# A softmax-free attention and a gated layer on one core: a PSUM bank opened one unit sooner, the loads of v one period later, one weight sum on another engine

## The chip, the cores and the metric

The kernel runs on one core of a Trainium2 chip. The metric is the time of one execution in device microseconds (us), as the median of several runs. A core has TensorE (PE in the profile, its weight loads PEld), VectorE (DVE), ScalarE (ACT), GpSimd (POOL) and SyncE (SP). SP, ACT and POOL issue DMA transfers, each in the order of its own queue; 16 DMA engines carry them out.

## The reference

The first half is a linear attention with decay over q, k and v of shape 4 x 8 x 768 x 64 (batch, heads, sequence, head size). Per head, with a decay `lam` near 1:

```python
intra = np.einsum('bhic,bhjc->bhij', qb, kb) * Dmask[None]   # Dmask: lam ** (i - j) for i >= j, else 0
intra = np.einsum('bhij,bhjd->bhid', intra, vb)
inter = np.einsum('bhid,bhde->bhie', qb * lam_pow[None], kv_state)
out[:, :, sl] = intra + inter
kv_state = lam_block * kv_state + np.einsum('bhsd,bhse->bhde', kb_dec, vb)
```

Its output, as 3072 tokens of 512, goes through a layer: `h = x @ w_in` (512 x 2048), `g = h * tanh(softplus(h))` (Mish), `g @ w_out` (2048 x 512). All inputs and the output are float32.

## The kernel before

**Staging.** The sequence is cut into 6 groups of 128 positions; a group holds four batch entries, so 512 tokens. A chunk, numbered i = 4 n + b, is one batch entry b of group n: k, q and v of 128 positions in 8 heads. `load_k`, `load_q` and `load_v` (lines 61 to 78) fetch a chunk through POOL's queue and convert it to float16. k and q have 8 buffers each; v has 8 fixed tiles `vz`, so group n shares its tiles with group n - 2. `scale_k` (L265) multiplies k by its decay to `ktil`; `turn` (L269) makes `ktil` and transposes q and `ktil` by DMA on SP's queue (L274, `qraw` and `kraw`).

**Periods and units.** The program is an order written out by hand: every engine works through its own instructions as the Python code emits them. Period n holds the layer of group n and, laid between its pieces, the attention of group n + 1. The unit is the piece of the layer's work. Period 0 has its own loop (L741), periods 1 to 5 that at L776. In a unit, the code first emits the unit's matmuls, then a load, sums on DVE, a turn, and the attention step that `visit` names.

- *Units 0 to 13 of periods 2 to 5* make h. `mm1_duo` (L422) computes a block of 2 x 128 features by 256 tokens with 8 matmuls into one of two `ph` banks, and ACT applies Mish (L441). Half 0 of the tokens is in units 0 to 5, half 1 in units 6 to 13. The last 512 features are computed as seven products of quarters and of their sums (`set_unit`, L506): P1 in unit 4, P2 in 5, P5 and P6 in 10, P7 and P3 in 12, P4 in 13. P5 has the bank `sw`; P6, P7 and P4 share `sz`; P3 has `sy`. The step `open` (L546) takes the banks of `sw` and `sz` and has ACT copy P1's result, kept in SBUF as `u1`, into `sz` (L548), onto which P6 adds. After P5 ACT keeps its result as `p5` (L539), and after P6 it copies `sz` to `sy` (L564). The seven sums of `x_sum` (four on DVE, L496) and `in_sum` are the operands.
- *The following 14 units* make the output: seven products again, two units each (`fast_unit`, L663), with operands `gsum` (L589) and `tsum` (L461). `tsum` is made once, in period 0, by `weight_sum`: four sums of quarters of w_out in two halves each, seven of these on DVE and the last, `weight_sum(3, 1)`, on POOL (L765). Period 1 has plain units 0 to 15 instead of 0 to 13, so its output is in units 16 to 29.

**PSUM.** Tags name banks: `ph` and `po` have two each, `pS`, `pk`, `pO` and `pq` one. `sw` and `sz` are the two `po` banks. So are, in unit 6, two of the four banks of scores of `pair_s` (L338); DVE frees them by masking the scores into `sb` (L365), those two first.

**The attention in the periods.** `pair_s` computes scores of two chunks of group n + 1 from `qraw` and `kraw` (L349), `pair_o` (L368) multiplies them with v (L376), scales them on DVE to `xtok` (L384) and transposes that by DMA on SP's queue to `xt` (L386), the layer's input of the next period. Chunks 0 and 1 are in units 6 and 14 and give half 0; chunks 2 and 3 are in units 24 and 27, and give half 1, which unit 6 of the next period reads. `pair_a` (units 3 and 19) updates the state. In period 0 `look_t`, `look_s` and `look_o` do the same with transposes on PE (L211), in the last 7 units; the transposes of k and one of the banks of scores share the bank `pk`.

**The loads.** In period 0, behind unit 25, 26 and 27, two loads each of group 2 are emitted; `scale_k(7)` on POOL stands behind those of unit 26. In period n = 1, 2, 3 the list `later` holds the twelve loads of group n + 2 and gives one at each unit of `slots`. Ahead of each, `pace` (L396) has POOL copy one element of what ACT wrote last, so that POOL can't run ahead.

Of the kernel before, what the change touches and what calls it, by code (L numbers as in the profile page):

```python
# [20 lines left out]
def kernel(  # L21
# [10 lines left out]
    nc = tc.nc  # L32
    B, H, S, D = q.shape
    C = 128
    NG = S // C
# [21 lines left out]
    def chunk_rows(t, i):  # L57
        n, b = divmod(i, B)
        return t[b, :, n * C : (n + 1) * C, :].rearrange("h p c -> p h c")
# [17 lines left out]
    def load_v(i):  # L77
        nc.gpsimd.dma_start(out=vz[i % NVB][:, :, 0:D], in_=chunk_rows(v, i))  # L78
# [218 lines left out]
    def look_kv(i, tag="po"):  # L297

        n, b = divmod(i, B)
        pv = ps.tile([128, JP, 128], F32, name="pv", tag=tag, bufs=2 if tag in ("po", "ph") else 1)  # L300
        for j in range(JP):
            nc.tensor.matmul(
                pv[:, j, :].rearrange("p (a e) -> p a e", a=2),
                ktil[i][:, 2 * j : 2 * j + 2, :].rearrange("p h c -> p (h c)"),
                vz[i % NVB][:, 2 * j : 2 * j + 2, 0:D],
                start=(j == 0), stop=(j == JP - 1), skip_group_check=True,
            )
        if n == 0:
            return lambda: nc.vector.tensor_tensor(out=wst[b], in0=pv, in1=lbm, op=ALU.mult)
        return lambda: sum_rows(n, b, pv, 0, JP, lambda rs: wst[b][rs, :, rs])  # L310
# [84 lines left out]
    def pace():  # L395
        nc.gpsimd.tensor_copy(paced, mark[-1])  # L396
# [49 lines left out]
    tsum = [const.tile([128, HK, HN], F16, name=f"tsum{i}") for i in range(4)]  # L446

    def w_quarter(r, c, s):

        return wout[2 * r + s][:, :, c * HN : (c + 1) * HN]  # L450

    def weight_sum(i, s, engine=None):

        ks = slice(s * NKI // WS, (s + 1) * NKI // WS)
        a, b, op = (
            (w_quarter(0, 1, s), w_quarter(0, 0, s), ALU.subtract),
            (w_quarter(1, 1, s), tsum[0][:, ks, :], ALU.subtract),
            (w_quarter(1, 1, s), w_quarter(0, 1, s), ALU.subtract),
            (w_quarter(1, 0, s), tsum[1][:, ks, :], ALU.subtract),
        )[i]  # L460
        (engine or nc.vector).tensor_tensor(out=tsum[i][:, ks, :], in0=a, in1=b, op=op)  # L461

    KH = NKC // 2
    SU = NKI - 4
# [109 lines left out]
    def token_sum(n, i, part):  # L574

        if (n, i) not in gsum:
            gsum[n, i] = work.tile([128, HK, 2 * C], F16, name=f"gsum{i}", tag=f"gsum{i}", bufs=1)
        w = HK // 2
        ks = slice(part * w, part * w + w)
        kh = slice(HK + part * w, HK + part * w + w)  # L580
        h = hsg[n]
        lo, hi = slice(0, 2 * C), slice(2 * C, 4 * C)
        a, b, op = (
            lambda: (h[:, ks, hi], h[:, kh, hi], ALU.add),
            lambda: (gsum[n, 0][:, ks, :], h[:, ks, lo], ALU.subtract),
            lambda: (h[:, ks, lo], h[:, ks, hi], ALU.subtract),
            lambda: (h[:, kh, lo], gsum[n, 1][:, ks, :], ALU.subtract),
        )[i]()
        nc.vector.tensor_tensor(out=gsum[n, i][:, ks, :], in0=a, in1=b, op=op)  # L589
# [146 lines left out]
    units = [(mm1_unit, (0, ni)) for ni in range(NKI)]  # L736
# [4 lines left out]
    for u, (fn, args) in enumerate(units):  # L741
        put_off = []
        fn(*args, **({"then": put_off} if u in (23, 25) else {}))
        if u < B - 1:
            look_kv(u + 1, "pq" if u == 0 else "po")()
        if 8 <= u < 8 + NVB - B:
            nc.vector.memset(vz[u - 8 + B][:, :, D : 2 * D], 0.0)
        elif u == 13:
            nc.vector.tensor_scalar(out=maskT, in0=rel, scalar1=0.0, scalar2=None, op0=ALU.is_ge)
        for i, s in {14: ((0, 0),), 15: ((0, 1),), 18: ((1, 0), (2, 0)),  # L750
                     20: ((1, 1), (2, 1))}.get(u, ()):
            weight_sum(i, s)
        for i, part in sums.get(u, ()):
            token_sum(0, i, part)
        if u == 8:
            for i in range(4):
                in_sum(i)
        if u == 22:
            scale_k(4)
            weight_sum(3, 0)  # L760
        then = [f(i, "po" if i == 5 else "ph") if f is look_kv else f(i) for f, i in visit.get(u, ())]
        if u == 23:
            scale_k(5)
            scale_k(6)
            weight_sum(3, 1, nc.gpsimd)  # L765
        for f in put_off + then:
            if f:
                f()
        if u in (25, 26, 27):
            for _ in range(2):  # L770
                ahead.pop(0)()
        if u == 26:
            scale_k(7)
    next_state(1, 0)

    for n in range(1, NG):  # L776
        r, s, t = Pair(), Pair(), Pair()
        r.n, r.bs, s.n, s.bs, t.n, t.bs = n, (2, 3), n + 1, (0, 1), n + 1, (2, 3)
        visit = {}
        d = 0 if n == 1 else 2  # L780
        if 1 < n < NG - 1:
            visit[3] = pair_a, r
        if n < NG - 1:
            visit[6 if d else 11] = pair_s, s
            visit[16 - d] = pair_o, s
            visit[26 - d] = pair_s, t
            visit[29 - d] = pair_o, t
        if n < NG - 2:
            visit[21 - d] = pair_a, s
        turns = {23 - d: (n + 2) * B, 25 - d: (n + 2) * B + 1}  # L790
        turns.update({3: (n + 1) * B + 2, 5: (n + 1) * B + 3} if d else {1: 9, 4: 10, 7: 11})

        def duo(g, half):
            return mm1_duo, (n, g, half * (GT // 2), (half + 1) * (GT // 2))

        def part(step):
            return set_unit, (n, step)

        if d:
            units = [[duo(g, 0)] for g in range(4)]  # L800
            units += [[part("P1"), duo(4, 0)], [part("P2"), duo(5, 0)]]
            units += [[duo(g, 1)] for g in range(3)] + [[duo(3, 1), part("open")]]
            units += [[part("P5"), part("P6")], [duo(4, 1)], [part("P7"), part("P3")], [duo(5, 1), part("P4")]]
        else:
            units = [[duo(g, half)] for half in range(2) for g in range(NKI // 2)]
        steps = ("P1", "P5", "P6", "P2", "P7", "P3", "P4")
        units += [[(fast_unit, (n, step, blk))] for step in steps for blk in range(2)]
        later = []
        if n < NG - 2:
            later = [(lambda f=f, i=(n + 2) * B + b: f(i)) for f, b in (  # L810
                (load_k, 0), (load_q, 0), (load_k, 1), (load_q, 1), (load_k, 2), (load_q, 2),
                (load_v, 0), (load_v, 1), (load_k, 3), (load_q, 3), (load_v, 2), (load_v, 3))]
        if d:
            slots = *range(6, 14), 15, 17, 19, 21
            sums = {13: ((0, 0), (0, 1), (1, 0), (1, 1)), 17: ((2, 0),), 18: ((2, 1),), 20: ((3, 0),), 21: ((3, 1),)}
        else:
            slots = *range(8, 16), 17, 19, 21, 23
            sums = {9: ((2, 0),), 11: ((2, 1),), NKI - 3: ((0, 0), (1, 0)), NKI - 1: ((0, 1), (1, 1)),
                    NKI + 4: ((3, 0),), NKI + 5: ((3, 1),)}
        for u, calls in enumerate(units):  # L820
            for fn, args in calls:
                fn(*args)
            if n == 1 and u == 0:
                turn(8)
                look_s(7)
            if n == 1 and u == 2:
                f = look_kv(7)
                look_o(7)
                f()
                next_state(1, 1)  # L830
            for _ in range({0: 1, 1: 1, 2: 2, 3: 1, 4: 1}.get(u, 0) if n == 1 else 0):
                pace()
                ahead.pop(0)()
            if later and u in slots:
                pace()
                later.pop(0)()
            for i, part in sums.get(u, ()):
                token_sum(n, i, part)
            if turns.get(u, NG * B) < NG * B:
                turn(turns[u])  # L840
            if d and u == 6:
                x_sum(n, 0)
            if u in visit:
                f, s_ = visit[u]
                s_.spare = ("po", "po") if u < 12 else ("pS", "pk") if f is pair_a else ("ph", "po")
                f(s_)
            if d and u == 6:
                for i in range(1, 4):
                    x_sum(n, i)
# [30 lines left out]
```

## Time and profile before

| | us |
|---|---|
| median of 3 runs | 205.01 (204.87 to 205.74) |
| the profiled execution | 206.21 |
| its span, from the first to the last instruction | 204.4 |
| PE busy | 191.2 (94%) |
| DVE busy | 141.8 (69%) |
| ACT busy | 99.0 (48%) |
| POOL busy | 82.2 (40%) |

The granted clock of PE is at full speed over the whole span. A row of the timeline has the start, the duration, engine and line, operation, what it writes and reads (`ph<-xt,win`), the shapes, the count, and in brackets how long the engine stood idle before it and what ended that. Rows with a count merge several instructions. Matmuls overlap, so a row of 8 matmuls that lasts 1.04 us gives way to the next after some 0.87. Starts are in us from the beginning of the span.

### The profile page before, as it was taken

Reading aid. Unit: us, or ns where it says so; the run is one execution under the profiler, and the core shown is the slowest. Engines: PE = TensorE matmul, PEld = TensorE weight load, DVE = VectorE, ACT = ScalarE, POOL = GpSimd, SP = SyncE. Lnnn points to the kernel's source line nnn. Section 1 sums busy time; section 2 is a strip of 40 time slices with the busy share of each in tenths; the row PEclk is TensorE's granted clock in tenths of the full one; section 3 lists DMA queues with packets and bytes.
Section 4 is the critical chain, followed back from the end, with each engine's and each line's share of the span. In section 5 each row is a group of like instructions: output and inputs, shape, how many; then the busy total and the mean of one; then the engine's idle time right before and its main releaser. Section 6 shows DMA issues by size and latency. Waiting matters only on the chain. (4 is left out here: it accounts for less than half of the span.)

```text
span 204.4 us, 5076 instructions
## 1 busy us (share of the span) xinstructions
PE 191.2 (94%) x2065; PEld 158.2 (77%) x2065; DVE 141.8 (69%) x278; ACT 99.0 (48%) x174; POOL 82.2 (40%) x130
## 2 busy tenths in 40 slices
PE   7778999997999999978999998999998999998993
PEld 3544447885888998967998987998987988987883
DVE  7888299795935978556699775699685777322913
ACT  5793674333565430556621466620567530667430
POOL 7995333879688952008772008772000000000000
PEclk9999999999999999999999999999999999999999
DMA  9999999999999999999999959999951023500014
GB/s 130 139 158 200 206 206 192 154 196 139 164 124 167 147 139 183 148 238 74 109 122 184 220 106 97 105 104 187 251 103 30 2 51 106 154 3 0 3 51 156
DMA packets 112458, 26.82 MB, mean 131 GB/s; under 512 B 101554, under 2 KB 112434, under 8 KB 112434
## 3 DMA queue, kind: packets, MB, share of 16 engines
q0 software_dynamic: 77552, 13.37, 92.6%
q1 hardware_dynamic: 30848, 9.97, 27.7%
q10 hardware_dynamic: 4034, 3.15, 4.9%
q8 instruction: 16, 0.26, 0.6%
q14 instruction: 8, 0.07, 0.1%
HBM read 27.26 MB, written 6.29 MB: 164 GB/s over the span
## 5 line engine op out<-in xcount | busy, mean ns | idle before, releaser
L434 PE MATMUL ph<-xt,win 128*128 128x256 f16 x512 | 60.5, 273 | 1.2 <-DMA xt<-xtok 1.2
L434 PEld LDWEIGHTS <-win 128*128 128x128 f16 x512 | 49.2, 98 | 7.3 <-DMA xt<-xtok 1.4
L441 ACT ACTIVATE hsg<-ph 128x512 f16<-128x512 f32 x64 | 38.1, 596 | 23.3 <-PE ph L434 23.3
L603 PEld LDWEIGHTS <-gsum 128*128 128x128 f16 x384 | 36.7, 98 | 5.1 <-DVE gsum L589 0.3
L603 PEld LDWEIGHTS <-hsg 128*128 128x128 f16 x272 | 26.1, 98 | 3.2
L603 PE MATMUL x<-wout,hsg 128*128 128x256 f16 x192 | 23.7, 273 | 0.0
L75 POOL DMA_DIRECT2D qn<-in_q_dram x23 | 20.4, 888 | 7.6 <-DMA wout<-in_moe_w_out_dram 3.4
L589 DVE TENSOR_TENSOR gsum<-hsg 128x1024 f16<-128x1024 f16 x24 | 15.8, 686 | 11.0 <-ACT hsg L441 7.2
L603 PE MATMUL z<-tsum,gsum 128*128 128x256 f16 x192 | 23.3, 273 | 0.0
L67 POOL DMA_DIRECT2D kn<-in_k_dram x23 | 20.5, 891 | 6.6 <-DMA win<-in_moe_w_in_dram 2.3
L78 POOL DMA_DIRECT2D vz<-in_v_dram x24 | 21.1, 882 | 4.1 <-DMA wout<-in_moe_w_out_dram 1.7
L365 DVE TENSOR_TENSOR sb<-pS,maskT 128x512 f16<-128x512 f32 x32 | 19.9, 682 | 3.8 <-PE pS L349 3.7
L396 POOL COPY paced<-hsg 1x1 f16<-1x1 f16 x33 | 7.7, 235 | 31.0 <-ACT hsg L441 29.9
L265 DVE TENSOR_TENSOR ktil<-kn,lk 128x512 f16<-128x512 f16 (+1 forms) x22 | 14.9, 682 | 2.8 <-DMA kn<-in_k_dram 2.8
L288 DVE TENSOR_TENSOR raw<-pv,state 64x256 f32<-64x256 f32 x24 | 10.1, 422 | 7.4 <-PE pv L328 6.8
L405 PE MATMUL ph<-xt,win 128*128 128x512 f16 x64 | 14.5, 379 | 0.7 <-DMA win<-in_moe_w_in_dram 0.7
L660 ACT ACTIVATE osum<-z 128x512 f32<-128x512 f32 x5 | 3.0, 597 | 23.7 <-PE z L603 23.7
L543 DVE TENSOR_TENSOR hs<-sz,p 128x512 f32<-128x512 f32 x4 | 2.8, 691 | 14.7 <-PE sz L553 14.7
L417 ACT ACTIVATE hsg<-ph 128x512 f16<-128x512 f32 x16 | 9.6, 597 | 6.3 <-PE ph L405 6.3
L603 PE MATMUL y<-wout,gsum 128*128 128x256 f16 x96 | 12.3, 273 | 0.0
L405 PEld LDWEIGHTS <-win 128*128 128x128 f16 x64 | 6.1, 98 | 7.8 <-DMA win<-in_moe_w_in_dram 1.2
L603 PE MATMUL w<-tsum,gsum 128*128 128x256 f16 x96 | 11.6, 273 | 0.0
(115 smaller groups left out, 269.5 us busy)
## 6 DMA issues: line engine op xcount, KB each, us to landing
vz<-in_v_dram POOLq DMA_DIRECT2D x24, 128.0 KB, 6.0
out_dram<-osum SPq DMA_DIRECT2D x12, 256.0 KB, 3.5
kn<-in_k_dram POOLq DMA_DIRECT2D x23, 128.0 KB, 5.9
qn<-in_q_dram POOLq DMA_DIRECT2D x23, 128.0 KB, 5.9
out_dram<-osum ACTq DMA_DIRECT2D x11, 256.0 KB, 3.8
wout<-in_moe_w_out_dram POOLq DMA_DIRECT2D x4, 512.0 KB, 17.0
win<-in_moe_w_in_dram POOLq DMA_DIRECT2D x3, 512.0 KB, 10.7
win<-in_moe_w_in_dram POOLq DMA_DIRECT2D x2, 256.0 KB, 6.8
```

The lines of the kernel that those rows point to most:

```text
L67: nc.gpsimd.dma_start(out=kn[i], in_=chunk_rows(k, i))
L75: nc.gpsimd.dma_start(out=qn[i], in_=chunk_rows(q, i))
L78: nc.gpsimd.dma_start(out=vz[i % NVB][:, :, 0:D], in_=chunk_rows(v, i))
L265: (nc.gpsimd if B + 1 < i < 2 * B else nc.vector).tensor_tensor(out=t, in0=kn[i], in1=bc(lk, 2, D), op=ALU.mult)
L288: nc.vector.tensor_tensor(out=raw[rs, b % 2, j0 : j0 + nj, :], in0=pv[rs, :, rs], in1=olds(rs), op=ALU.add)
L365: nc.vector.tensor_tensor(out=s.sb[m][t], in0=sc[m][t], in1=bc(maskT, 1, JP), op=ALU.mult)
L405: nc.tensor.matmul(ph_t[ni][:, lo:hi], w_in(ni, kc), xt[n][:, kc, lo:hi], start=(kc == 0), stop=(kc == NKC - 1),)
L417: nc.scalar.activation(hsg[n][:, ni, :], ph_t.pop(ni), AF.Mish)
L434: nc.tensor.matmul(t[:, m, lo - half * h : hi - half * h], w_in(ni, kc), xt[n][:, kc, lo:hi], start=(m == 0 and kc == 0), stop=(kc == NKC ...
L441: nc.scalar.activation(hsg[n][:, 2 * g : 2 * g + 2, half * h : half * h + h], t, AF.Mish)
L589: nc.vector.tensor_tensor(out=gsum[n, i][:, ks, :], in0=a, in1=b, op=op)
L603: nc.tensor.matmul(places(n, key)[:, blk, lo:hi], lhs(kk, blk), rhs(kk, lo, hi), start=(fresh and kk == 0 and blk == 0), stop=(kk == HK - ...
```

## The change

Three edits:

1. `open` stands in unit 8, ahead of the matmuls and the Mish of that unit's `duo`; before, it stood in unit 9 behind them.
2. `weight_sum(3, 1)` in unit 23 of period 0 is on DVE, not on POOL.
3. `later` of period n = 1, 2, 3 keeps the eight loads of k and q of group n + 2, chunk by chunk, in consecutive units (8 to 15 of period 1, 6 to 13 of periods 2 and 3). The four loads of v of group n + 1 stand in units 1 to 4 of periods n = 2, 3, 4. Before, all twelve of group n + 2 were in one period, and units 15 or 17 to 21 or 23 had the last four.

```diff
-    def weight_sum(i, s, engine=None):
+    def weight_sum(i, s):
...
-        (engine or nc.vector).tensor_tensor(out=tsum[i][:, ks, :], in0=a, in1=b, op=op)
+        nc.vector.tensor_tensor(out=tsum[i][:, ks, :], in0=a, in1=b, op=op)
...
-            weight_sum(3, 1, nc.gpsimd)
+            weight_sum(3, 1)
...
-            units += [[duo(g, 1)] for g in range(3)] + [[duo(3, 1), part("open")]]
+            units += [[duo(0, 1)], [duo(1, 1)], [part("open"), duo(2, 1)], [duo(3, 1)]]
...
         later = []
+        if 1 < n < NG - 1:
+            later += [lambda i=(n + 1) * B + b: load_v(i) for b in range(B)]
         if n < NG - 2:
-            later = [(lambda f=f, i=(n + 2) * B + b: f(i)) for f, b in (
-                (load_k, 0), (load_q, 0), (load_k, 1), (load_q, 1), (load_k, 2), (load_q, 2),
-                (load_v, 0), (load_v, 1), (load_k, 3), (load_q, 3), (load_v, 2), (load_v, 3))]
+            later += [lambda f=f, i=(n + 2) * B + b: f(i) for b in range(B) for f in (load_k, load_q)]
         if d:
-            slots = *range(6, 14), 15, 17, 19, 21
+            slots = *range(1, 5), *range(6, 14)
...
         else:
-            slots = *range(8, 16), 17, 19, 21, 23
+            slots = range(8, 16)
```

## The prediction

> **What bounds the kernel now.** I read the waits of TensorE (PE) first, then the timeline around each of them. The columns of the waits are: who waited for whom, us in total, times, longest.
>
> ```profile
> core 0 of [0], span 204.4 us
> engine line waited for: us in total, times, longest us
> PE sz L553 <- ACT sz L548: 3.0, 4, 0.7
> PE pk L211 <- POOL ktil L265: 1.5, 1, 1.5
> PE ph L434 <- DMA xt<-xtok: 1.2, 1, 1.2
> ```
>
> PE is the bound: little else holds it up, and behind the start these three are the largest waits, 5.7 us together. Each edit touches one: the opened bank the first, the moved sum the second, the moved loads the third. What else the edits do is worked out beside them. An engine's own busy total says nothing here: the 5.7 us sit in six places of PE's order.
>
> **Edit 1, the bank.** The wait of 3.0 us is four waits of 0.74, one in each of the periods 2 to 5. Here it is in period 3, on ScalarE (ACT), PE and VectorE (DVE).
>
> ```profile
> 123.32 0.60 ACT L441 ACTIVATE hsg<-ph 128x512 f16<-128x512 f32 x1 [1.17 <-PE ph L434]
> 124.19 0.60 ACT L441 ACTIVATE hsg<-ph 128x512 f16<-128x512 f32 x1 [0.28 <-PE ph L434]
> 125.06 0.60 ACT L441 ACTIVATE hsg<-ph 128x512 f16<-128x512 f32 x1 [0.28 <-PE ph L434]
> 125.56 0.60 ACT L548 ACTIVATE sz<-u 128x512 f32<-128x512 f32 x1
> 126.08 0.59 ACT L539 ACTIVATE p<-sw 128x512 f32<-128x512 f32 x1
> 126.89 0.58 ACT L564 ACTIVATE sy<-sz 128x512 f32<-128x512 f32 x1 [0.22 <-ACT p L539]
> ```
>
> ```profile
> 124.86 0.60 PE L553 MATMUL sw<-xsum,isum 128*128 128x256 f16 x4
> 126.20 0.60 PE L553 MATMUL sz<-xsum,isum 128*128 128x256 f16 x4 [0.74 <-ACT sz L548]
> 126.64 1.04 PE L434 MATMUL ph<-xt,win 128*128 128x256 f16 x8
> 127.52 0.60 PE L553 MATMUL sz<-xsum,isum 128*128 128x256 f16 x4
> ```
>
> ```profile
> 122.10 2.48 DVE L365 TENSOR_TENSOR sb<-pS,maskT 128x512 f16<-128x512 f32 x4 [0.88 <-PE pS L349]
> 124.50 0.41 DVE L496 TENSOR_TENSOR xsum<-xsum,xt 128x512 f16<-128x512 f16 x1
> ```
>
> P5 starts at 124.86 and takes 0.44 (126.20 to 126.64 is the same size), so P6 could start at 125.30. It waits for the copy into its bank, 125.56 to 126.16, which stands on ACT behind the Mish of unit 9. In the new order it stands ahead of the Mish of unit 8 and can start when the Mish of unit 7 ends, 123.92. It adds one wait: its bank is one of the two that the attention scores hold until DVE has masked them. The first two of the four masks free the pair, at 122.10 + 2.48 / 2 = 123.34, before 123.92, so that wait costs nothing. If it did cost, the Mish of units 8 and 9 would queue behind it on ACT, and PE would wait for their banks at unit 11. The copy runs 123.92 to 124.52; the Mish of unit 8 starts at 124.52 in place of 124.19, and its bank is wanted at 125.74 by unit 11, after it ends (125.12). P6's other operand is ready at 124.91. So P6 starts at 125.30 and nothing hides that.
>
> What is late next: P7 writes the bank that the copy into y reads. P7 would come at 125.30 + 0.44 + 0.88 = 126.62 (8 matmuls take 127.52 - 126.64). On ACT p5 starts at 125.06 + 0.50 = 125.56, the copy into y at 125.56 + 0.52 = 126.08, and ends at 126.66; a release takes 0.04 (126.16 to 126.20), so P7 starts at 126.70, 0.1 late. **Gain 0.74 - 0.1 = 0.64 a period, 2.56 in four.** Bounds: 3.0, if P7 isn't late, and 0.4 a period, 1.6, if ACT's copies keep a quarter more.
>
> **Edit 2, the sum.** At the end of period 0, POOL makes ktil, then the sum, then issues four loads, then makes the last ktil, which PE awaits.
>
> ```profile
> 43.30 2.12 POOL L461 TENSOR_TENSOR tsum<-wout,tsum 128x1024 f16<-128x1024 f16 x1
> 45.37 0.95 POOL L67 DMA_DIRECT2D kn<-in_k_dram  x1
> ```
>
> ```profile
> 48.93 1.08 POOL L265 TENSOR_TENSOR ktil<-kn,lk 128x512 f16<-128x512 f16 x1
> ```
>
> ```profile
> 40.47 1.05 PE L603 MATMUL z<-tsum,gsum 128*128 128x256 f16 x8
> 41.36 0.39 PE L211 MATMUL pk<-ident,ktil 128*128 128x128 f16 x4
> ```
>
> ```profile
> 47.52 1.05 PE L603 MATMUL z<-tsum,hsg 128*128 128x256 f16 x8
> 50.07 0.40 PE L211 MATMUL pk<-ident,ktil 128*128 128x128 f16 x4 [1.50 <-POOL ktil L265]
> ```
>
> ```profile
> 40.58 1.29 DVE L239 TENSOR_TENSOR sb<-pS,maskT 128x512 f16<-128x512 f32 x2
> ```
>
> ```profile
> L461 DVE TENSOR_TENSOR tsum<-wout,tsum x3: 682/685/692, 34.5 to 38.0; 128x1024 f16<-128x1024 f16 x3
> ```
>
> Removed on POOL: 2.07 (45.37 - 43.30), so the last ktil ends at 50.01 - 2.07 = 47.94, and PE, free at 47.52 + 0.88 = 48.40, would not wait: 50.07 - 48.40 = 1.67 gone. Added on DVE: 0.69 ahead of the masks at 40.58. They are not covered: the transposes at 41.36 write the bank that the first mask frees, 40.58 + 0.65 = 41.23, a slack of 0.1. PE therefore runs about 0.64 later from 41.36 on (0.69 less the slack) and reaches the last transposes at 49.04. **Gain 1.67 - 0.64 = 1.03.** Bounds: 1.67, if DVE's shift is absorbed, and 0, if what follows isn't ready earlier.
>
> That can be: in period 1, PE goes from matmuls straight into the scores, whose operand has just landed.
>
> ```profile
> 63.45 0.62 PE L349 MATMUL pS<-qraw,kraw 64*128 64x128 f16 x16
> ```
>
> ```profile
> L274 SPq DMA_TRANSPOSE kraw<-ktil x2: 1193/1216/1239, 54.0 to 56.7; - x2
> ```
>
> ```profile
> DMA to landing us min/median/max: 4.9/6.8/6.8
> ```
>
> The second kraw lands at 56.7 + 6.8 = 63.5, just on time. Its chain begins with loads that POOL issues 2.07 earlier, and its DVE steps follow PE, so I take it to move by the same 1.03; if not, 1.03 is given back (a rival).
>
> **Edit 3, the loads of v.** The number of loads and of paced copies stays; POOL has no other work in periods 1 to 4, so its 0.9 us an issue costs nothing by itself. What counts is the traffic beside the transposes of xt (SyncE's queue), whose second half is wanted at unit 6.
>
> ```profile
> 90.18 1.03 PE L434 MATMUL ph<-xt,win 128*128 128x256 f16 x8 [1.19 <-DMA xt<-xtok]
> ```
>
> ```profile
> 119.60 1.91 PE L434 MATMUL ph<-xt,win 128*128 128x256 f16 x16
> ```
>
> ```profile
> 149.91 1.91 PE L434 MATMUL ph<-xt,win 128*128 128x256 f16 x16
> ```
>
> ```profile
> 115.84 0.60 ACT L441 ACTIVATE hsg<-ph 128x512 f16<-128x512 f32 x1 [0.28 <-PE ph L434]
> ```
>
> These rows are unit 6 of period 2, units 5 and 6 of periods 3 and 4 (so unit 6 at 120.48 and 150.79), and the Mish of unit 1 of period 3. Next are the transposes that periods 2, 3 and 4 await: their time on SyncE's queue (min/median/max) and first and last start, with the landing where it is used. Of the last two, each a landing alone, the first is that of the v load issued at 77.1, the second that of the transposes at 133.9, amid loads.
>
> ```profile
> L386 SPq DMA_TRANSPOSE xt<-xtok x2: 1218/2101/2984, 83.0 to 86.1; - x2
> ```
>
> ```profile
> L386 SPq DMA_TRANSPOSE xt<-xtok x2: 1212/1214/1216, 115.9 to 117.2; - x2
> ```
>
> ```profile
> DMA to landing us min/median/max: 2.5/2.6/2.8
> ```
>
> ```profile
> L386 SPq DMA_TRANSPOSE xt<-xtok x2: 1218/1683/2148, 145.3 to 147.5; - x2
> ```
>
> ```profile
> DMA to landing us min/median/max: 10.0/10.0/10.0
> ```
>
> ```profile
> DMA to landing us min/median/max: 5.7/5.7/5.7
> ```
>
> In period 2 the DMA engines are behind: the v of 77.1 lands at 87.1, and the first transpose stands 2.98 on its queue in place of 1.22. Period 1 now issues 8 loads in units 8 to 15, and none later; so I take the queue to be drained, and the second transpose to start at 86.1 - (2.98 - 1.22) = 84.3. PE wants it at 90.18 - 1.19 = 88.99. But four v loads now come in units 1 to 4 of periods 2, 3 and 4, where there were none: in period 3 from 115.84 + 0.60 = 116.4 on, beside the second transpose. With a landing L the second transposes are late by L - 4.7 in period 2, L - 3.3 in period 3 (120.48 - 117.2) and L - 3.3 in period 4 (150.79 - 147.5), or nothing. No row shows L beside such loads; the nearest are 2.6 without and 5.7 amid them. In the latter, loads had been running all along; here at most two are issued before the second transpose has left its queue. I take a third of the way, L = 3.6: late by 0, 0.3, 0.3. **Gain 1.2 - 0.6 = 0.6.** Bounds: 1.2 (L up to 3.3), and a loss of 4.6 (L = 5.7: 1.0 + 2.4 + 2.4 = 5.8, less 1.2). The v are used at unit 14 and later, so their own landing costs nothing, even at 10.0.
>
> **Sum:** 2.56 + 1.03 + 0.6 = 4.2. The span goes from 204.4 to 200.2; the profiled execution took 206.21, some 1.8 around the span, and would take 202.0. The median of the runs, 205.01, is below that; applied to it: **200.8**.
>
> **Rivals.**
> 1. Transposes and loads share the engines evenly, so that each transpose beside a load lands in twice its time alone, L = 5.2. Late: 0.5 + 1.9 + 1.9 = 4.3, less 1.2 now: a loss of 3.1, and 3.6 - 3.1 = 0.5 is gained: 204.5. For it: 5.7 is over twice 2.6. Against it: the v come late beside the transposes. The Trainium skill, "DMA: Bandwidth & Descriptors", section "Queues, rings and completion order", says that each engine round-robins between the queue rows that have work, packet by packet; by that rule this rival holds wherever a load stands beside a transpose all along, and the rows 2.6 and 5.7 agree.
> 2. **Slower:** the four v loads, issued in a row, hold the second transposes longer than loads do now. From L = 5.7 on the loss of 4.6 exceeds the 3.6 by 1.0 us. At L = 6.5: 1.8 + 3.2 + 3.2 = 8.2, and 8.2 - 1.2 - 3.6 = 3.4 is lost: 208.4. For it: 5.7 exists already, with loads 1 us apart. Against it: in period 3 the first transpose has gone before the first v is issued.
> 3. Edit 2 is eaten by kraw in period 1 (above): 201.8.
> 4. P6 starts earlier, but ACT doesn't: P7 takes over 0.5 of the 0.74. Four times 0.4 are lost against the forecast: 202.4. Against it: ACT has 1.17 idle ahead of 123.32.
>
> **How the numbers follow.** Forecast 0.58, rival 1 0.16, rival 2 0.10, rival 3 0.10, rival 4 0.06. A measurement of this kernel can't tell less than about 0.5% (1.0 us) from no change. Faster by more: forecast and rivals 3 and 4, 0.74; within: rival 1, 0.16; slower: rival 2, 0.10. Low end: all upper bounds, 3.0 + 1.67 + 1.2 = 5.9, from 205.0 is 199.1. The high end takes in rival 1: 204.6; outside is rival 2 and a little on each side. The forecast's own range is 199.1 to 202.6.
>
> **What would show it.** Edit 1: no wait of sz for ACT's L548, the copy two units earlier on ACT, and a wait at P7 of 0.1 in its place. Edit 2: no wait of pk for POOL; DVE's sb near 41.3; PE in the period 1 scores about 1 us earlier, without a wait for kraw. Edit 3: no wait of ph for xt in period 2, and less than 0.5 in periods 3 and 4. The prediction is wrong if ph waits for xt in three periods (L above 5), if ACT's copy waits for sb, or if PE stands before the scores of period 1.

## The result, and the profile after

| us | before | after |
|---|---|---|
| median | 205.18 (204.39 to 206.65, 22 runs) | 203.35 (200.93 to 207.15, 22 runs) |
| the profiled execution | 206.21 | 201.19 |
| its span | 204.4 | 199.4 |

The ratio is 0.9865, with a 95% interval of 0.9838 to 0.9891, so about 2.8 us less. It leaves out runs over 1.5% above a kernel's fastest; of the 22 of after these are eight, most likely long by this kernel's own waits (below), and by the medians of all runs the change is worth 1.8 us. The forecast was 200.8, 4.2 us less. The direction was right, the size was not: 1.4 to 2.4 us are missing, and the times after scatter over 6 us, where before they scatter over 2.

The waits of PE in after (engine and line, for whom, us in total, times, longest):

```profile
core 0 of [0], span 199.4 us
engine line waited for: us in total, times, longest us
...
PE ph L434 <- ACT hsg L441: 0.7, 1, 0.7
...
PE pk L211 <- DVE sb L239: 0.4, 1, 0.4
```

All three waits of the prediction are gone. Two new ones stand in their place: 0.4 for DVE's masks, and 0.7 that the list puts down to ACT. Each step can be followed in the timeline.

**Edit 1**, the same place in period 3, on ACT and on PE:

```profile
119.88 0.60 ACT L441 ACTIVATE hsg<-ph 128x512 f16<-128x512 f32 x1 [1.17 <-PE ph L434]
120.37 0.60 ACT L548 ACTIVATE sz<-u 128x512 f32<-128x512 f32 x1
120.89 1.33 ACT L441 ACTIVATE hsg<-ph 128x512 f16<-128x512 f32 x2
122.12 0.59 ACT L539 ACTIVATE p<-sw 128x512 f32<-128x512 f32 x1
122.60 0.61 ACT L564 ACTIVATE sy<-sz 128x512 f32<-128x512 f32 x1
```

```profile
121.43 0.60 PE L553 MATMUL sw<-xsum,isum 128*128 128x256 f16 x4
121.86 0.60 PE L553 MATMUL sz<-xsum,isum 128*128 128x256 f16 x4
122.30 1.04 PE L434 MATMUL ph<-xt,win 128*128 128x256 f16 x8
```

The copy L548 now stands behind the Mish of unit 7 and starts without waiting for a mask. P6 comes 0.43 behind P5 (121.86 - 121.43) and has no wait. P7 could start at 122.30 + 0.88 = 123.18, and this row has it at 123.25, 0.07 late:

```profile
123.25 0.60 PE L553 MATMUL sz<-xsum,isum 128*128 128x256 f16 x4
```

So 0.74 - 0.07 = 0.67 is gained in the period; the forecast had 0.64.

**Edit 2**, the end of period 0 on DVE, then three rows of PE:

```profile
40.46 0.68 DVE L461 TENSOR_TENSOR tsum<-wout,tsum 128x1024 f16<-128x1024 f16 x1
41.06 1.28 DVE L239 TENSOR_TENSOR sb<-pS,maskT 128x512 f16<-128x512 f32 x2
```

```profile
41.80 0.38 PE L211 MATMUL pk<-ident,ktil 128*128 128x128 f16 x4 [0.40 <-DVE sb L239]
...
47.96 1.05 PE L603 MATMUL z<-tsum,hsg 128*128 128x256 f16 x8
48.84 0.39 PE L211 MATMUL pk<-ident,ktil 128*128 128x128 f16 x4
```

The sum stands ahead of the masks, PE waits 0.40 for them at the first transposes, and the last transposes follow the matmuls at once (47.96 + 0.88 = 48.84): the 1.50 for POOL is gone. They come 1.23 earlier than before (50.07 - 48.84). PE was 0.12 ahead already at the matmuls in front of the first transposes (40.35, before 40.47), so edit 2 gives 1.11 by the trace, forecast 1.03. Is it given back in period 1? The first matmul of that period and its scores are at 50.18 and 62.20 after, 51.42 and 63.45 before: 12.02 and 12.03 apart. The second kraw came earlier with everything else.

```profile
50.18 1.04 PE L434 MATMUL ph<-xt,win 128*128 128x256 f16 x8
...
62.20 0.62 PE L349 MATMUL pS<-qraw,kraw 64*128 64x128 f16 x16
```

**Edit 3**, period 4, where the 0.7 of the list stands. First DVE, then PE, then the time of the two transposes of xt on SP's queue (min/median/max, first and last start) and their landing:

```profile
147.37 0.43 DVE L496 TENSOR_TENSOR xsum<-xt 128x512 f16<-128x512 f16 x1 [0.41 <-DMA xt<-xtok]
```

```profile
147.41 1.03 PE L434 MATMUL ph<-xt,win 128*128 128x256 f16 x8 [0.72 <-ACT hsg L441]
```

```profile
L386 SPq DMA_TRANSPOSE xt<-xtok x2: 1219/1503/1787, 141.0 to 142.9; - x2
DMA to landing us min/median/max: 4.0/4.2/4.4
```

The bracket at 147.41 names ACT. But DVE waited for a transpose of the same xt until 147.37, and the transposes say the same: 142.9 + 4.4 = 147.3. PE waited for xt. Such a wait is read with the neighbour's bracket, not with its own alone.

### The profile page after: what moved, and what is told of

It is laid out like the page before. It is cut to its first block, busy times and chain, and to the rows that moved or that the text cites. A ratio compares the mean times of both kernels' runs of the same rounds, so it can differ in the third digit from the quotient of the medians.

```text
span 199.4 us, 5087 instructions
## 1 busy us (share of the span) xinstructions
PE 191.5 (96%) x2065; PEld 159.1 (80%) x2065; DVE 142.3 (71%) x279; ACT 98.2 (49%) x174; POOL 78.8 (40%) x129
## 4 chain that ended last, share of the span: by engine, by line
PE 91%; ACT 4%; DMA 2%; DVE 2%; issue 1%; ACTq 0%
PE ph L434 28%; PE z L603 14%; PE x L603 11%; PE ph L405 7%; PE y L603 6%; PE w L603 5%; PE sz L553 3%; PE pS L349 2%; PE pO L376 2%; PE pO L255 2%; PE sx L553 2%; DMA kn<-in_k_dram 2%; PE pv L328 1%; PE pS L234 1%; PE pk L211 1%; PE pO L357 1%
## 5 line engine op out<-in xcount | busy, mean ns | idle before, releaser
L396 POOL COPY paced<-hsg 1x1 f16<-1x1 f16 x42 | 9.6, 229 | 47.8 <-ACT hsg L441 47.6
L384 DVE TENSOR_TENSOR xtok<-pO,lqt 128x256 f16<-128x256 f32 x32 | 11.3, 413 | 0.2
```

The costliest lines, as they stand in the source:

```text
L384: nc.vector.tensor_tensor(out=xtok[m][:, :, t, :], in0=s.pO[t][:, m], in1=bc(lt[:, :, t], 2, D), op=ALU.mult)
```

## The experiments

Two questions were open: what each edit gives by itself, and why edit 3 gives less than nothing. The theory for the second is that the four loads of v delay the second transposes of xt. The rivals are that what was taken for a gain of edit 3 (the 1.2 us wait in period 2) isn't there in most executions, and that edits 1 and 2 give less than they seem to, in which case edit 3 is innocent.

### Each edit alone

Edit 1 alone (e1_open):

```diff
-            units += [[duo(g, 1)] for g in range(3)] + [[duo(3, 1), part("open")]]
+            units += [[duo(0, 1)], [duo(1, 1)], [part("open"), duo(2, 1)], [duo(3, 1)]]
```

> Edit 1 alone (the bank opened one unit sooner). By the prediction the four waits of sz for ACT's L548 (3.0 us) vanish and P7 keeps about 0.1 each: 2.5 us faster than before, a ratio of 0.988, with a spread of the runs like that of the kernel before (some 2 us). Rival (whatever gains time on PE also gets a wider spread, since the cause lies with PE's own pace or the clock): the waits vanish all the same in the profile, but the runs spread over some 6 us and the ratio is above 0.992.

Measured: 201.81 (201.15 to 202.92) beside 204.84, ratio 0.9837 (0.9802 to 0.9872), 3.0 to 3.3 us less. Nothing is lost to the scores' masks or to P7. Its waits of PE, and unit 5 and 6 of period 2 with their transposes:

```profile
PE pk L211 <- POOL ktil L265: 1.3, 1, 1.3
...
PE ph L405 <- DMA win<-in_moe_w_in_dram: 0.3, 1, 0.3
```

```profile
88.45 1.91 PE L434 MATMUL ph<-xt,win 128*128 128x256 f16 x16
```

```profile
L386 SPq DMA_TRANSPOSE xt<-xtok x2: 1217/1224/1230, 83.5 to 84.8; - x2
```

The wait of sz is gone, that for POOL, which edit 2 removes, is left. The loads here are those of before, and yet units 5 and 6 of period 2 run through, 16 matmuls in one row, and the transposes take 1.2 us on the queue. In the profile of before it was 2.98, and PE waited 1.19.

Edit 2 alone (e2_sum):

```diff
-            weight_sum(3, 1, nc.gpsimd)
+            weight_sum(3, 1)
```

> Edit 2 alone (the last w_out sum on DVE). By the prediction PE enters period 1 about 1.0 us earlier and keeps it: ratio 0.995. Rival: PE then stands before the scores of period 1 for kraw, and the wait of ph for xt in period 2 grows by what was gained, since the DMA engines and not PE set when that transpose lands: ratio 1.000, with that wait near 2.2 in place of 1.2.

Measured: 204.19 (203.42 to 205.76) beside 204.84, ratio 0.9960 (0.9938 to 0.9983), so 0.3 to 1.3 us less. The waits are as expected, and period 2 has no wait for xt in this profile either:

```profile
PE sz L553 <- ACT sz L548: 3.0, 4, 0.7
...
PE ph L405 <- DMA win<-in_moe_w_in_dram: 1.1, 1, 1.1
...
PE pk L211 <- DVE sb L239: 0.4, 1, 0.4
```

```profile
87.45 1.91 PE L434 MATMUL ph<-xt,win 128*128 128x256 f16 x16
```

The wait for w_in stands ahead of the first matmul of h in period 0, near 17 us, where no edit reaches: 0.3 in e1_open, 0.7 in before, 1.1 here. Up to one us of the scatter between executions can come from there.

Edit 3 alone (e3_loads): the third edit's lines of the diff above, `later` and `slots`.

> Edit 3 alone (the loads of v a period later). By the prediction the wait of ph for xt in period 2 (1.2) goes, and 0 to 0.7 come in periods 3 and 4: 0.6 us faster, ratio 0.997, and if the landing beside the loads differs from run to run, this kernel has the wide spread of the changed one (some 6 us) while edits 1 and 2 alone have not. Rival (the spread comes with a busier PE): a narrow spread here.

Measured: 206.45 (205.26 to 211.32) beside 204.84, ratio 1.0054 (1.0031 to 1.0078): slower, by 1.1 us and more. Two rows of its profile, unit 6 of periods 3 and 4:

```profile
120.18 1.03 PE L434 MATMUL ph<-xt,win 128*128 128x256 f16 x8 [0.22 <-DMA xt<-xtok]
...
150.81 0.93 PE L434 MATMUL ph<-xt,win 128*128 128x256 f16 x7 [0.16 <-DMA xt<-xtok]
```

The waits are where the prediction put them, and about as long as it said; but this execution took 206.25, and 211.3 was measured twice. One profile doesn't show what an edit does whose cost varies from execution to execution. A second profile of it, and one of the whole change, stand below.

### Edit 3 left out

Edits 1 and 2 (e5_open_sum), and the same kernel once more (e11_open_sum): the diff above without its part 3.

> Edits 1 and 2 together, without the moved loads. If edit 3 is what takes time back, this kernel is faster than the changed one and as narrow as edit 1 alone: the ratios of edits 1 and 2 alone multiply to 0.9837 x 0.996 = 0.980, about 200.8 us, and the changed kernel at 0.9865 lies 1.3 us above it. If instead the edits hinder each other (a busier PE), the ratio is 0.985 or more and the loads cost nothing more.

> The kernel with edits 1 and 2 only, again, on the same chip. Expected 200.6 us, within 0.5 us of the one with v behind unit 6: then edit 3 has nothing to gain in a typical execution, and the 1.2 us that it was to save stood only in the profiled one.

Measured: 200.59 (200.18 to 200.96) beside 204.77, ratio 0.9798 (0.9778 to 0.9818); then 201.26 (200.45 to 201.48) beside 204.83, ratio 0.9809 (0.9781 to 0.9836). The product of edits 1 and 2 alone is 0.9837 x 0.9960 = 0.9798: the gains add up. This is 2.1 to 2.8 us below the median of the 22 runs of after, and 1.3 below after timed side by side with the second (e12_after, below). Its times scatter over 1 us or less (four and five runs); those of after over 6 in 22 runs, and over 2.9 in the six of e12_after. Units 5 and 6 of period 4 run through (profile of e5_open_sum). The longest landing below, 3.6, is that of the first transpose (141.7 + 3.6 = 145.3); the second took 2.5, so it lands at 143.2 + 2.5 = 145.7, and unit 6 begins at 146.36 + 0.87 = 147.23, 1.5 later.

```profile
L386 SPq DMA_TRANSPOSE xt<-xtok x2: 1221/1320/1420, 141.7 to 143.2; - x2
DMA to landing us min/median/max: 2.5/3.1/3.6
```

```profile
146.36 1.91 PE L434 MATMUL ph<-xt,win 128*128 128x256 f16 x16
```

### The loads of v moved past the transposes, and ahead of them

All edits, but the loads of v in units 6 and 7, two each (e4_v_behind; again as e10_v_behind):

```diff
-            slots = *range(1, 5), *range(6, 14)
+            slots = 6, 6, 7, 7, 8, 8, 9, 9, 10, 11, 12, 13
...
-            if later and u in slots:
+            for _ in range(min(len(later), tuple(slots).count(u))):
```

> All three edits, but the four loads of v stand in units 6 and 7, two each, behind the transposes that unit 6 awaits, and k and q follow up to unit 13. If the loads beside the transposes of xt cost the changed kernel its time and its spread, PE waits for xt in no period, the median is 1 to 2 us below that of the changed kernel (about 201.5, ratio 0.982) and the spread is narrow. If they don't, the ratio stays at 0.986 with the same spread.

> The kernel with v behind unit 6 again, on the same chip as the changed kernel and the one without edit 3. Expected 200.7 us; if moving four loads out of period 1 is worth anything once they stand clear of the transposes, it is at least 0.5 us below the kernel without edit 3.

Measured: 200.77 (200.27 to 201.13) beside 204.84, ratio 0.9786 (0.9759 to 0.9812); again 200.76 (200.43 to 201.10) beside 204.83, ratio 0.9798 (0.9773 to 0.9822). The same loads in the same period cost nothing that can be measured once they stand behind unit 5. The second, timed side by side with e11_open_sum, is 0.5 us below it, with intervals that overlap: spreading the loads gains nothing that can be measured.

The other way, two each in units 0 and 1 (e6_v_ahead):

```diff
-            slots = *range(1, 5), *range(6, 14)
+            slots = 0, 0, 1, 1, *range(6, 14)
```

> The changed kernel with the four loads of v issued earlier, two each in units 0 and 1 of periods 2 to 4 instead of one each in units 1 to 4, so that more of them stand beside the second transpose of xt. If the landing of that transpose is what counts, PE waits for xt in all three periods, 1 to 3 us each, and the median is 2 to 6 us above that of the changed kernel (205 to 209). If the loads hurt by anything else (the later turns, or POOL's queue), it stays within 1 us of the changed kernel.

Measured: 205.77 (204.82 to 209.60) beside 204.77, ratio 1.0043 (1.0006 to 1.0080). All that edits 1 and 2 gain is gone, and more. PE waits for xt in periods 2, 3 and 4, 5.6 us in all; below the sum are the waits of periods 3 and 4 (that of period 2 is 1.11).

```profile
PE ph L434 <- DMA xt<-xtok: 5.6, 3, 2.5
```

```profile
122.15 1.03 PE L434 MATMUL ph<-xt,win 128*128 128x256 f16 x8 [1.99 <-DMA xt<-xtok]
```

```profile
154.29 1.80 PE L434 MATMUL ph<-xt,win 128*128 128x256 f16 x8 [2.49 <-DMA xt<-xtok]
```

From v behind the transposes to v ahead of them, the wait goes from none to 5.6 us. In periods 2 and 3 some loads of k and q differ in place too, by one or two units, but in both kernels they stand behind unit 5; period 4 has no loads but the four of v, and its wait goes from none to 2.49. That the loads delay the transposes is shown by this pair.

### A second profile of after and of edit 3 alone

> The changed kernel once more, for a second look at one execution. Its waits of ph for xt in periods 2 to 4 should account for its distance from 200.8 us (what is expected without the loads), within 0.8 us for the start; if it comes out long with these waits short, the cause lies elsewhere.

> Edit 3 alone once more, for a second look. Its runs lay near 206.3 and near 211.3. A long one should show PE standing before unit 6 of one or more periods for xt by some 5 us in all; a short one has waits of 0.4 to 1.5 us there. If a long one shows no such wait, the landing is not what makes it long.

One profiled execution each. After took 204.0 here (e7_after_again), and its two waits at unit 6, of periods 3 and 4, are 0.77 and 2.03; the transposes stand below the second.

```profile
150.22 1.03 PE L434 MATMUL ph<-xt,win 128*128 128x256 f16 x8 [2.03 <-DMA xt<-xtok]
```

```profile
L386 SPq DMA_TRANSPOSE xt<-xtok x2: 1225/1708/2190, 142.5 to 144.8; - x2
DMA to landing us min/median/max: 3.7/4.5/5.3
```

144.8 + 5.3 = 150.1: the landing sets the start. 204.0 less the two waits is 201.2, a time as without edit 3. The profile of after with its 0.72 gives 201.19 - 0.72 = 200.5, and that of e12_after (below), with waits of 0.70 and 0.62, gives 202.94 - 1.32 = 201.6. So in these three profiles most of the spread of after is that of the waits; the longer runs, from 204.5 up, have no profile.

Edit 3 alone took 209.56 (e8_loads_again), with waits of 0.77 and 2.27 (its page puts the first down to ACT, as above), 3.0 in all where about 5 had been expected, and something else behind the second; see the last section.

### Half the bytes of v, and after beside it

The loads of v of groups 3 to 5 fetch four of eight heads (e9_half_v); this kernel leaves the other half of v out. After was timed side by side with it (e12_after).

```diff
-        nc.gpsimd.dma_start(out=vz[i % NVB][:, :, 0:D], in_=chunk_rows(v, i))
+        hs = H if i < 3 * B else H // 2
+        nc.gpsimd.dma_start(out=vz[i % NVB][:, 0:hs, 0:D], in_=chunk_rows(v, i)[:, 0:hs, :])
```

> The changed kernel, but the loads of v of groups 3 to 5 fetch only the first four of the eight heads (the other half of v stays that of an older group, so this part of the computation is left out). The same four issues in units 1 to 4, half the packets. If the packets beside the second transpose of xt make it late, the wait of period 4 falls from 0.7 to 2.0 us to at most 0.5 and the median is within 1 us of the kernel without edit 3 (200.6 to 201.6). If the issues on POOL or the start of a queue make it late, it stays at the changed kernel's 203.

> The changed kernel on the same chip: 202.5 to 203.5 us, 2 to 3 us above the two kernels before it, with a spread of over 4 us.

Measured: 201.92 (201.66 to 202.66), ratio 0.9859 (0.9835 to 0.9884), and after 202.54 (201.89 to 204.79), ratio 0.9899 (0.9857 to 0.9940), both beside 204.83. Neither expectation is met. Between after and e10_v_behind, timed with these two, lie 1.8 us, not 2 to 3, and after scatters over 2.9 us, not over 4. With half the bytes the time is 0.6 lower than that of after, but the intervals of the two ratios overlap, and it falls between the two outcomes that had been named. In the profile with half the bytes a line of code more shifts the numbers by one:

```profile
148.25 0.92 PE L435 MATMUL ph<-xt,win 128*128 128x256 f16 x7 [0.60 <-DMA xt<-xtok]
```

```profile
L387 SPq DMA_TRANSPOSE xt<-xtok x2: 1231/1678/2124, 142.0 to 144.2; - x2
DMA to landing us min/median/max: 3.7/3.8/3.9
```

The landing is 3.9 at most, and short waits (0.65 and 0.60) are left. The profile of e12_after, with all the bytes, has nearly the same waits, 0.70 in period 3 and 0.62 in period 4, with landings of 3.8 and 4.1:

```profile
149.18 1.03 PE L434 MATMUL ph<-xt,win 128*128 128x256 f16 x8 [0.62 <-DMA xt<-xtok]
```

So this pair doesn't show whether the delay goes with the bytes or with the four issues.

What makes one execution of after land at 4.4 and another at 5.3 can be read from the profiles: the moment at which the first load of v is issued, beside the start of the second transpose. Here are the first loads of periods 3 and 4 of after, and of period 4 of e7_after_again; the second transposes start at 113.28, 142.90 and 144.81 (the end of the two on SP's queue, less the second's time there).

```profile
113.93 0.87 POOL L78 DMA_DIRECT2D vz<-in_v_dram  x1 [0.63 <-PE ph L434]
```

```profile
143.12 0.87 POOL L78 DMA_DIRECT2D vz<-in_v_dram  x1 [0.34 <-PE ph L434]
```

```profile
144.62 0.87 POOL L78 DMA_DIRECT2D vz<-in_v_dram  x1 [0.34 <-PE ph L434]
```

The load is 0.65 behind, 0.22 behind and 0.19 ahead, and the landings are 2.5, 4.4 and 5.3. The same for all profiles:

| first load of v, from the start of the second transpose | where | landing of the second transpose, us |
|---|---|---|
| none in units 0 to 5 | periods 3 and 4 of before, e1_open, e2_sum, e5_open_sum, e11_open_sum, e4_v_behind, e10_v_behind | 2.4 to 2.6 |
| 0.57 to 1.08 behind | period 2 of after, e7_after_again, e12_after, e3_loads, e8_loads_again; period 3 of after | 2.4 to 2.5 |
| 0.07 ahead to 0.29 behind | period 3 of e7_after_again, e12_after, e3_loads, e8_loads_again; period 4 of after, e12_after, e3_loads | 3.6 to 4.4 |
| 0.18 to 1.31 ahead | period 4 of e7_after_again, e8_loads_again; periods 2 to 4 of e6_v_ahead | 5.1 to 5.4 |
| half the bytes, 0.44 and 0.12 ahead | periods 3 and 4 of e9_half_v | 3.7 and 3.9 |

A few tenths of a microsecond in the order of the two go with 1 to 3 us of landing, and in the three profiles of after period 2 doesn't wait, where the loads come 0.65 or more behind. Without these loads period 2 has 2.4 to 2.7, but 4.0 in before and 3.6 in e1_open, so they aren't all that delays a transpose. The 3.7 of e9_half_v, 0.44 ahead, lies below all the whole loads that come ahead by 0.18 or more, which speaks for the bytes. This is read off after the fact: no run moved the first load by tenths and nothing else, and what the four issues cost apart from their bytes stays open.

## Why the prediction was right in direction and wrong in size

1. **What bounds the kernel.** PE and the three waits: right for two. The third, 1.2 us for xt in period 2, stood in the one profiled execution, and not in the profiles of e1_open, e2_sum, e5_open_sum and e11_open_sum, which have the same loads. The numbers had said so: 206.21 - 1.19 = 205.02 is the median of the runs on which the forecast was built, 205.01. The prediction applied all of its gain to the median, though the median already lacked that wait.
2. **Edit 1** was forecast at 2.56. By itself it brings 3.0 to 3.3 us, by the trace 0.67 a period, 2.7. Each row came as worked out: no mask in the way, the copy behind the Mish of unit 7, P7 late by 0.07 for 0.1. Rival 4 (P7 takes over 0.5) is out.
3. **Edit 2** was forecast at 1.03. By itself it brings 0.7 us (0.3 to 1.3), and on top of edit 1 1.2 or 0.6 (201.81 less 200.59 or 201.26, which were not timed side by side); by the trace of after it is 1.11. The step 1.67 - 0.64 was right, the wait for DVE's masks is 0.40, and rival 3 (kraw eats it) is out: 12.02 beside 12.03. Edits 1 and 2 together: forecast 3.6, measured 4.2 and 3.6.
4. **Edit 3** was forecast as a gain of 0.6; it costs. This is the term that failed, and its sign with it. By itself it costs 1.1 us and more, within the whole 1.3 (202.54 - 201.26, timed side by side) to 2.8 (203.35 - 200.59, not so). Its two halves failed apart. The 1.2 saved isn't there in most executions (point 1). And the landing L, taken as "a third of the way" from 2.6 to 5.7, measured in period 4, was 4.4 in the profile of after, 4.1 in e12_after, 5.3 in e7_after_again and 5.2 in e8_loads_again. L = 3.6 is what e3_loads has (it waits 0.22 and 0.16); it is the shortest of the five in period 4. The step that failed is to take L as one number: it goes from 2.5 to 5.3 with the moment of the first load of v. By the prediction's own rows that load stands 0.8 ahead of the second transpose of period 3 (116.4 and 117.2), and 0.83 ahead e6_v_ahead landed in 5.1; that the loads came later than so in after and e3_loads kept the loss of period 3 small, and the prediction hadn't worked that out.
5. **The rivals.** Rival 1 has the mechanism where its condition holds, that a load stands beside the transpose all along: L = 5.2 is twice 2.6, and the second transposes whose first load of v was issued 0.18 or more ahead landed in 5.1 to 5.4, beside 2.4 to 2.6 without. It gave 1.9 of lateness in period 4, and 2.03 stood there in e7_after_again. The section of the Trainium skill named in the prediction ("DMA: Bandwidth & Descriptors", section "Queues, rings and completion order": DMA engines go round the queue rows that have work) agrees with these landings. But rival 1 was worked out for all executions and periods 2, 3 and 4, and period 2 doesn't wait in after. Rival 2 (slower) needed landings from 5.7 up; the longest measured is 5.4, in e6_v_ahead, which is slower than before all the same: there PE waits in period 2 too, the saved 1.2 is missing, and a long wait costs more than its length (last section).
6. **Seen in the profile.** The prediction named as its own refutation ph waiting for xt in three periods with L above 5. After waits in one period or in two, 0.6 to 2.0 us at a time, with L from 3.8 to 5.3: less than that refutation, more than the forecast's 0.3. The median of 203.35 lies outside the forecast's own range, 199.1 to 202.6, and inside the whole range only because that takes in rival 1.

The version that beats both is the change without its third part, or all three with the loads of v in units 6 and 7: 0.9786 to 0.9809 of the time before, about 4 us less.

## What to carry to other kernels

A wait that one profile shows is worth its length only if the runs have it: where the profiled execution is longer than the median by just that wait, its removal isn't to be counted against the median. A load that has slack of its own can still be the cause of a wait, if it shares the DMA engines with a transfer that has none; so place loads by the transfers next to them, here behind the last transpose that PE awaits, not where their queue is free. And an edit whose cost varies between executions shows itself as scatter, so compare the spread of the times (2.9 us in e12_after, 0.7 and 1.0 in the two kernels timed with it) as well as their middle.

## What the runs showed of the hardware

Two stands of PE, of 2.3 and 2.5 us, cost more than their length. These are stretches of one us behind the wait of 2.27 in e8_loads_again: busy share of PE, PEld, DVE, ACT and POOL, granted clock of PE, DMA share, GB/s.

```profile
151.00:152.00 1.00, 0.00 (x0) 0.00 (x0) 0.00 (x0) 0.02 (x1) 0.51 (x1) 1.00 1.85 146
152.00:153.00 1.00, 0.34 (x2) 0.28 (x3) 0.39 (x1) 0.00 (x0) 0.00 (x0) 0.71 1.98 148
153.00:154.00 1.00, 1.00 (x7) 0.70 (x5) 0.04 (x1) 0.00 (x0) 0.00 (x0) 0.50 2.54 176
154.00:155.00 1.00, 1.00 (x15) 0.59 (x15) 0.00 (x0) 0.44 (x1) 0.00 (x0) 0.50 2.37 127
155.00:156.00 1.00, 1.00 (x28) 0.90 (x25) 0.48 (x1) 0.15 (x1) 0.00 (x0) 0.58 1.62 207
156.00:157.00 1.00, 1.00 (x11) 0.90 (x10) 1.00 (x3) 0.07 (x1) 0.00 (x0) 1.00 0.97 101
```

PE stands from 150.39 to 152.66. The clock is full until about 152.4 and half from there to about 155.8 (0.58 us of the slice at 152, two whole slices, 0.84 us of that at 155: 3.4 us), most of which is work. From unit 6 to P5 it then took 5.82 us, in after 4.39: 1.4 us on top of the wait. The wait of 2.49 in e6_v_ahead was followed by the same, 5.93 us; stands of 1.99 (period 3 of e6_v_ahead) and 2.03 (e7_after_again) left the clock at 1.00:

```profile
149.00:150.00 1.00, 0.00 (x0) 0.00 (x0) 0.00 (x0) 0.00 (x0) 0.03 (x1) 1.00 1.76 144
150.00:151.00 1.00, 0.78 (x8) 0.71 (x8) 0.42 (x1) 0.00 (x0) 0.00 (x0) 1.00 2.15 155
```

The Trainium skill, "TensorE: Matmul & The Clock Gate", section "Part 1: The HAM clock gate (the "warmup" mystery)", puts the fall to half speed behind an idle window of about 3.4 us that runs on its own count. The 3.4 us at half speed here have the length of that window; the idle time that sufficed, 2.3 us, is shorter, and there the measurement decides. Length alone doesn't decide either: in e8_loads_again the clock fell some 2.0 us into the stand, and the stand of 2.03 left it full.

The longest runs, 205.83 to 207.15 of after and the two of 211.3 of e3_loads, have no profile. But each run's mean granted clock is known: 0.992 in these six, 0.997 to 1.000 in all other runs of those two kernels. 3.4 us at half speed in some 205 lower the mean by 0.008 (3.4 / 2 / 205). So the clock fell in them as well; that a late xt brought it down is argued, not shown.
